# One transformer block on one core: where a weight half is loaded, which engine reads a norm first, how a turned tile lies in PSUM, and how the last tile is stored

## The chip, the cores and the metric

The kernel runs on one core of a Trainium2 chip, in one launch. The metric is the device time of one execution in microseconds; of several runs the median is given. The profile is of one execution, taken apart by engine: TensorE (PE for its matmuls, PEld for its weight loads, which overlap them), VectorE (DVE), ScalarE (ACT), GpSimd (POOL), and SyncE (SP), which here only issues DMA transfers.

## The reference, cut to what matters

One block with 2048 tokens of width 576: a modulated layer norm, linear attention with 32 heads of width 18 and a two-sided softmax feature map, a gated residual; then a second modulated norm, a feed-forward of width 4608 with a relu, and a gated residual.

```python
mod = (silu(c) @ w_mod).reshape(1, 6, 1, -1)
sa, ca, ga, sb, cb, gb = (mod[:, i] for i in range(6))
h = layernorm(x) * (1 + ca) + sa
# attention, per head: q, k, v = h @ wqkv
pq, pk = q @ w_phi, k @ w_phi
phi_q = concat([softmax(pq), softmax(-pq)]);  phi_k = concat([softmax(pk), softmax(-pk)])
kv, z = phi_k.T @ v, phi_k.sum(over tokens)
o = (phi_q @ kv) / (phi_q @ z + 1e-6)
x = x + ga * (o @ wo)
h = layernorm(x) * (1 + cb) + sb
x = x + gb * (relu(h @ w1) @ w2)
```

## The kernel before

The tokens are 16 tiles of 128. The first phase is a list of short jobs, issued in a fixed order that is written down as a string of words. A word is a job, the number of its tile or chunk, and after a colon the pair of PSUM banks it uses (`Q12:3`: query projection of tile 12 into bank pair 3). Each engine does its own jobs in the order of the words. The ones the text speaks of:

- `K`, `V`, `Q`: projections (10 matmuls each); `eK`, `eQ`: the exponentials (ScalarE) that evacuate them; `sK`, `rK`, `pA`, `pM`, `vE`, `kv`: the key side; `FQ..`, `QR..`: folding the feature weights into the query weights, and their bias rows
- `sq`, `qi`: spill of a query tile to DRAM, and its reload; `qs`, `qp`, `qt`: its sums (VectorE), its second half (GpSimd), its turning by DMA
- `ga`, `gac`, `gaw`, `gar`: the attention gate as a row, written to DRAM and read back to all partitions; `wo`: the output weight times this row (GpSimd, five chunks)
- `nu`, `nO`, `ot`, `oc`: attention numerator of tile 0 or 1, its division, its turning and evacuation; `W`: output projection with the residual added
- `lb`, `lr`, `ap`: statistics, inverse deviation and application of the second norm; `xc`: copy of the residual out of PSUM; `ht`, `hd`, `ha`: turning of the normed tile, and evacuation with scale and shift by VectorE and ScalarE
- `wl`, `w2a`, `w2b`: loads of the feed-forward weights

The end of the string, where the query tiles and the first two attention tiles meet, reads before the change:

```python
... nu0:3 eQ6 Q7:2 sq5 nO0 sq4 nu1:1 eQ7 ot0:0 w2b1 nO1 Q8:3 oc0 Q9:2 eQ8 sq7 W0:1
eQ9 sq8 ot1:0 sq6 lb0 xc0 Q10:3 oc1 w2b0 lr0 Q11:2 eQ10 ap0 W1:0 eQ11 sq10 w2b2 ht0:1 lb1 xc1 Q12:3 ha0 hd0
lr1 Q13:2 eQ12 ap1 qi3 Q14:1 eQ13 sq11 ht1:0 sq12 Q15:3 ha1 hd1 sq13 eQ14 sq9 sq14 qi4 eQ15 sq15
```

The query tiles share six buffers, so tile 15 takes that of tile 9 after its spill; the reload `qi3` takes the buffer of tile 10:

```python
SLOT = (0, 1, 2, 3, 4, 5, 0, 1, 2, 3, 4, 5, 0, 1, 2, 3)
EL = carve(RT, RTL, (NL, 2 * D))          # its first two buffers are slots 4 and 5
def q_out(u): sp.dma_start(eqd[:, u, :], EQ[:, SLOT[u], :])
def q_in(u):  sp.dma_start(EL[:, u % NL, :], eqd[:, u, :])
def exps(t, pr, E):                       # eQ: two of them for each tile
    for s in range(2):
        act.activation(out=..., in_=pr[:, :, 0:HD]..., func=ACT.Exp, scale=rs[:, t, s:s + 1])
```

The second half of the second weight lies in a buffer `R2[1]` which first holds the transposed x of tiles 0 to 7:

```python
XOFF[t0 + j] = (R2[1], off, nt, j) if t0 < 8 else (RT, ...)      # x^T, 5120 of 10368 columns
def w2b_part(k):                                                  # three loads
    c = slice(6 * k * D, 6 * (k + 1) * D)
    sp.dma_start(R2[1][:, c], a["w2b"][:, c])
```

Turning and evacuating a normed tile:

```python
def turn(src, pr):
    pt = bf(pr[:, 0, :])                                          # one bank
    for ci in range(NC):
        pe.transpose(pt[:, ci * P:(ci + 1) * P], src[:, ci * P:(ci + 1) * P], ident[:, 0:P])

def h2_e(i, pr, eng):
    pt = bf(pr[:, 0, :])
    for ci in range(NC):
        o, p = h2[:, 0, ci, i * P:(i + 1) * P], pt[:, ci * P:(ci + 1) * P]
        if ci % 2 and eng is act:
            act.activation(out=o, in_=p, func=ACT.Identity, scale=..., bias=...)
        elif ci % 2 == 0 and eng is dve:
            dve.tensor_scalar(out=o, in0=p, scalar1=..., scalar2=..., op0=ALU.mult, op1=ALU.add)
```

The second phase is eight blocks of two tiles. Each has a first layer (`l1`, three groups of weight columns, each in three steps whose PSUM pairs 0, 1, 2 are evacuated by relus on ScalarE and VectorE) and a second layer (`l2`, seven products of 18 matmuls, a Strassen-like form). Attention and norm of the next two tiles run between their matmuls. The relus and the end of the last block:

```python
def relu(js, u):
    act.activation(out=A11[:, j, :], in_=lo[:, :, 0, :], func=ACT.Relu)
    act.activation(out=A2[:, j, :, :], in_=..., func=ACT.Relu)
    dve.scalar_tensor_tensor(out=U3[:, j, :], in0=lo[:, :, 1, :], scalar=0.0, in1=A11[:, j, :], op0=ALU.max, op1=ALU.subtract)
...
    fin(t + 1, 0, X, None)
    sp.dma_start(outf[(t + 1) * P:(t + 2) * P, :], x_sb[:, t + 1, :])
    prod(Z, A12, B22, al)
    if b + 1 < NB:
        fin(t, 1, Z, 1)
    else:
        y, z, c = yt[:, 0, :], yt[:, 1, :], slice(HD, D)
        pool.tensor_tensor(out=z, in0=SS[:, 1, :], in1=gb_row[:, c], op=ALU.mult)
        pool.tensor_tensor(out=z, in0=z, in1=x_sb[:, t, c], op=ALU.add)
        dve.tensor_tensor(out=y, in0=PS[:, Z, 0:HD], in1=gb_row[:, c], op=ALU.mult)
        dve.tensor_tensor(out=x_sb[:, t, c], in0=y, in1=z, op=ALU.add)
    sp.dma_start(outf[t * P:(t + 1) * P, :], x_sb[:, t, :])
```

Of the kernel before, what the change touches and what calls it, by code (L numbers as in the profile page):

```python
# [7 lines left out]
P = 128  # L8
# [14 lines left out]
NX = X0 + 4  # L23
NJ = DFF // P
HD = 288
G6 = ((0, 6), (6, 6), (12, 4), (16, 6), (22, 6), (28, 4))
GR = 108
GP = 112
# [12 lines left out]


ORDER = """
Z11 sx sd rp sc FK ca Z2 fra2 fsr frd4 fra1 sh fs1 frr fra0 bn0 fs3 bn1 fra3 fs0 Z1 shc sa0 wsd1 KR:0 fsd4 fs2
sp0 bn3 T0:2 VR:1 Tc0 bn2 KRh Ka0:2 KRd sa2 wsd0 sp2 VRh Kb0 wsd3 Ka1:0 wsd4 eKa0 VRd Kb1 wsd2 T2:1 eKa1 sK0
V0:2 Tc2 sK1 FQ1:0 rK0 K3:1 FQra1 pA0 FQs1 pM0 vE0 eK3 K2:0 bn4 bn5 rK1 kv0 eK2 m2:2 pA1 sK3 pM1 sa4 V1:1 sK2
m2c rK3 sp4 FQ3:0 V3:2 pA3 vE1 FQs3 pM3 FQra3 bn6 kv1 rK2 T4:1 V2:0 vE3 Tc4 pA2 bn7 pM2 K4:1 vE2 sa6 bn8 K5:2
eK4 sp6 bn10 T6:0 kv2 Tc6 ga:1 eK5 sK4 K6:0 gac bn9 rK4 V4:2 eK6 pA4 sK5 pM4 K7:1 sa8 vE4 rK5 gb:0 sK6 eK7 pA5
V5:2 sp8 gaw pM5 wl1 bn11 gbc T8:1 rK6 FQ0:0 kv3 Tc8 FQrd0 kv4 sa10 K8:1 pA6 vE5 FQs0 pM6 sK7 kv5 eK8 FQ4:2
V7:0 gar FQrd4 gbw sp10 w2a2 rK7 sK8 K9:1 FQs4 pA7 pM7 vE7 rK8 V6:2 eK9 bn13 gbr wl0 wo2 V8:0 vE6 sK9 pA8 kv6  # L50
kv7 pM8 V9:1 vE8 rK9 bn12 w2a0 T10:2 FQ2:0 pA9 Tc10 kv8 FQrd2 pM9 sa12 K10:2 vE9 FQs2 bn15 QR:1 w2a1 eK10 sp12
K11:0 bn14 wo3 QRh kv9 QRe eK11 V11:2 sK10 wo0 QRd wl3 sa14 T12:1 sK11 wo1 V10:0 Tc12 rK10 pA10 K12:1 rK11
sp14 vE10 pA11 Q0:0 pM10 vE11 eK12 wl4 K13:2 eQ0 sK12 pM11 wl2 kv10 eK13 V13:1 qs0 wo4 rK12 kv11 T14:0 V12:2
sK13 pA12 Tc14 pM12 K14:0 vE12 rK13 pA13 kv12 eK14 vE13 pM13 K15:2 V14:1 sK14 eK15 qp0 kv13 rK14 V15:0 sK15
qt0 pA14 pM14 Q1:2 vE14 rK15 Q2:1 eQ1 pA15 vE15 pM15 kv14 eQ2 Q3:0 qs1 kv15 sq2 eQ3 Q4:2 tp1 qp1 kz sq3 Q5:1
eQ4 qt1 tp0 Q6:0 eQ5 tp2 qi2 nu0:3 eQ6 Q7:2 sq5 nO0 sq4 nu1:1 eQ7 ot0:0 w2b1 nO1 Q8:3 oc0 Q9:2 eQ8 sq7 W0:1
eQ9 sq8 ot1:0 sq6 lb0 xc0 Q10:3 oc1 w2b0 lr0 Q11:2 eQ10 ap0 W1:0 eQ11 sq10 w2b2 ht0:1 lb1 xc1 Q12:3 ha0 hd0
lr1 Q13:2 eQ12 ap1 qi3 Q14:1 eQ13 sq11 ht1:0 sq12 Q15:3 ha1 hd1 sq13 eQ14 sq9 sq14 qi4 eQ15 sq15
"""

@with_exitstack
def tile_block(ctx, tc, a, out):
    nc = tc.nc
    outf = out.flatten_outer_dims()
# [49 lines left out]
    ident = small([P, P + 1], BF16, "ident")  # L114
# [9 lines left out]
    gb_row = small([P, D], BF16, "gb_row")  # L124
# [11 lines left out]
    sc = small([P, 4, NX], BF16, "sc")  # L136
# [19 lines left out]
    PS = psum.tile([P, 8, 512], FP32, name="PS")  # L156
# [6 lines left out]
    act, dve, pool, sp, pe = nc.scalar, nc.vector, nc.gpsimd, nc.sync, nc.tensor  # L163

    def bf(ap):
        return ap.bitcast(BF16)

    XOFF = {}
    off = 0
    for t0, nt in BLK:  # L170
        for j in range(nt):
            XOFF[t0 + j] = (R2[1], off, nt, j) if t0 < 8 else (RT, off - 8 * NC * P + xT_hi, nt, j)
        off += NC * nt * P

    def xt(t, ck, n=1):
# [277 lines left out]

    w1a = carve(R1, 0, (4, DFF))
    w1b = R1[:, 4 * DFF:]
    NK = NJ // 2
    w2 = [carve(R2[i], 0, (NK, D)) for i in range(2)]
    B11, B21, B22 = w2[0][:, :, 0:HD], w2[1][:, :, 0:HD], w2[1][:, :, HD:D]
    B12, T3 = w2[0][:, :, HD:D], carve(R2[0].bitcast(FP16), 0, (NK, D))[:, :, HD:D]
    RTh = RT.bitcast(FP16)  # L460
    T1, T2, T4 = (carve(RTh, i * TW, (NK, HD)) for i in range(3))
# [3 lines left out]
    A12, A22 = A2[:, :, 0, :], A2[:, :, 1, :]  # L465
    SS = RS[:, 0:6 * HD].bitcast(FP32).rearrange("p (a f) -> p a f", f=HD)
    X, Y, Z = 6, 4, 7
# [58 lines left out]
    def turn(src, pr):  # L526
        pt = bf(pr[:, 0, :])
        for ci in range(NC):
            pe.transpose(pt[:, ci * P:(ci + 1) * P], src[:, ci * P:(ci + 1) * P], ident[:, 0:P])

    def h2_e(i, pr, eng):
        pt = bf(pr[:, 0, :])
        for ci in range(NC):
            o, p = h2[:, 0, ci, i * P:(i + 1) * P], pt[:, ci * P:(ci + 1) * P]
            if ci % 2 and eng is act:
                act.activation(out=o, in_=p, func=ACT.Identity, scale=mod2[:, 1, ci:ci + 1], bias=mod2[:, 0, ci:ci + 1])
            elif ci % 2 == 0 and eng is dve:
                dve.tensor_scalar(out=o, in0=p, scalar1=mod2[:, 1, ci:ci + 1], scalar2=mod2[:, 0, ci:ci + 1],  # L538
                                  op0=ALU.mult, op1=ALU.add)

# [2 lines left out]
        sp.dma_start(R2[0][:, c], a["w2a"][:, c])  # L543

    def w2b_part(k):
        c = slice(6 * k * D, 6 * (k + 1) * D)
        sp.dma_start(R2[1][:, c], a["w2b"][:, c])

    def w1_part(i):
# [39 lines left out]
    def k_minus(t):  # L589
# [9 lines left out]
    at = {}  # L599
# [12 lines left out]
                                         in1=ca1[0:R, :].unsqueeze(2).to_broadcast([R, NC, FW]), op=ALU.mult),  # L612
# [23 lines left out]
        "W": lambda i: wo_mm(i, at["W", i], True), "lb": lambda i: ln2_bn(i, at["W", i]), "lr": ln2_rs,  # L636
        "xc": lambda i: act.activation(out=v2(x_sb[:, i, :]), in_=at["W", i][:, :, 0:HD], func=ACT.Copy),
        "ap": lambda i: ln2_apply(i, at["W", i]),
        "ht": lambda i: turn(xn[:, i, :], at["ht", i]),
        "hd": lambda i: h2_e(i, at["ht", i], dve), "ha": lambda i: h2_e(i, at["ht", i], act),  # L640
        "tp": lambda k: t_part(0, k),
    }
# [70 lines left out]
    def fin(t, k, bank, s):  # L713

        c = slice(k * HD, (k + 1) * HD)
        y = yt[:, k, :]
        if s is None:
            dve.tensor_tensor(out=y, in0=PS[:, bank, 0:HD], in1=gb_row[:, c], op=ALU.mult)  # L718
        else:
            dve.tensor_tensor(out=y, in0=PS[:, bank, 0:HD], in1=SS[:, s, :], op=ALU.add)  # L720
            pool.tensor_tensor(out=y, in0=y, in1=gb_row[:, c], op=ALU.mult)  # L721
        pool.tensor_tensor(out=x_sb[:, t, c], in0=y, in1=x_sb[:, t, c], op=ALU.add)  # L722

    def l2(b, hooks):
# [24 lines left out]
        copy(1)
        prod(Z, A11, T1, lo, True)  # L750
        prod(X, U3, T3, al)
        copy(2)
        prod(Z, A11, T1, hi)
        if b == 0:
            dve.tensor_tensor(out=A12, in0=A12, in1=U2, op=ALU.subtract)
        fin(t + 1, 1, Z, 2)
        prod(X, A22, T4, al)
        fin(t + 1, 0, X, None)
        sp.dma_start(outf[(t + 1) * P:(t + 2) * P, :], x_sb[:, t + 1, :])
        prod(Z, A12, B22, al)  # L760
        if b + 1 < NB:
            fin(t, 1, Z, 1)
        else:
            y, z, c = yt[:, 0, :], yt[:, 1, :], slice(HD, D)
            pool.tensor_tensor(out=z, in0=SS[:, 1, :], in1=gb_row[:, c], op=ALU.mult)
            pool.tensor_tensor(out=z, in0=z, in1=x_sb[:, t, c], op=ALU.add)
            dve.tensor_tensor(out=y, in0=PS[:, Z, 0:HD], in1=gb_row[:, c], op=ALU.mult)
            dve.tensor_tensor(out=x_sb[:, t, c], in0=y, in1=z, op=ALU.add)
        sp.dma_start(outf[t * P:(t + 1) * P, :], x_sb[:, t, :])

    NB = NT // 2
    for b in range(NB):
        t0 = 2 * b + 2
# [144 lines left out]
```

The softmax here doesn't subtract the row's maximum and nothing guards it: scores larger than these inputs give would overflow.

## Time and profile before

| | before |
|---|---|
| time, median of 3 runs | 395.94 us (395.25 to 397.05) |
| span of the profiled execution | 396.0 us |
| first layer of block 0 starts | 96.88 us |
| second layer of block 0 starts | 117.57 us |
| last matmuls end | 391.9 us |
| `w2b` loads, x count, size, median time to land | x3, 864 KB, 8.5 us |
| spills of query tiles | x14, 288 KB, 3.6 us |
| stores of output tiles | x16, 144 KB, 1.7 us |

The page gives busy time per engine first. Matmuls overlap one another, so a stretch in which PE shows as busy throughout may still hold slow spots: the distance between the starts of equal pieces tells more than the busy share. In a timeline a piece is a run of equal instructions, with the idle time of its engine ahead of it and what ended that idle time in brackets. A wait matters only if TensorE, which has next to no idle time, stands at the end of it. The DMA list gives the time from issue to landing; issues on the sync queue go out in order, so one that must wait holds back all behind it.

### The profile page before, as it was taken

To read this page: it belongs to the slowest core of one execution; us is meant where nothing else is said; L and a number is where in the kernel's file an instruction comes from. 1 tells how busy PE (TensorE), PEld (TensorE's weight loads), DVE (VectorE), ACT (ScalarE), POOL (GpSimd) and SP (SyncE) were. 2 spreads that over 40 slices of the span, in tenths; PEclk is the share of its full clock that TensorE was granted. 3 is DMA by queue.
4 is the path that set the end of the run, shared out by engine and by line. 5 is a ranking of instruction groups with operands and counts; after the bars stand their busy time and mean duration, and the time that the engine had idled before them with its cause. 6 is when DMAs were issued, how large, how long until landed. Compare 5 with 4: busy or idle time off the path is not lost.

```text
span 396.0 us, 8920 instructions
## 1 busy us (share of the span) xinstructions
PE 384.5 (97%) x3698; PEld 311.1 (79%) x3698; DVE 243.8 (62%) x452; ACT 157.6 (40%) x360; POOL 141.6 (36%) x199
## 2 busy tenths in 40 slices
PE   7999999998899999999999999999999999999995
PEld 3778888876687888788878888887888778878884
DVE  0799997845489845754657376557655755654221
ACT  1788877787441053113312411341053113312510
POOL 2145889600201420651074026404520651072045
PEclk9999999999999999999999999999999999999999
DMA  8999777398641142025212411341141045110000
GB/s 233 346 390 362 259 278 290 91 304 289 190 104 34 31 106 65 18 59 118 25 33 62 108 36 31 88 73 29 40 98 35 17 56 63 26 34 31 2 0 31
DMA packets 49468, 44.41 MB, mean 112 GB/s; under 512 B 39362, under 2 KB 41907, under 8 KB 48915
## 3 DMA queue, kind: packets, MB, share of 16 engines
q1 hardware_dynamic: 49154, 43.66, 39.0%
q8 instruction: 29, 0.48, 0.5%
q10 hardware_dynamic: 272, 0.18, 0.2%
q14 instruction: 13, 0.10, 0.1%
HBM read 28.03 MB, written 6.49 MB: 87 GB/s over the span
## 4 chain that ended last, share of the span: by engine, by line
PE 78%; DMA 7%; POOL 7%; ACT 3%; DVE 2%; issue 2%; SPq 0%; POOLq 0%; ACTq 0%; DVEq 0%
PE PS L676 31%; PE PS L735 29%; PE PS L273 6%; PE PS L683 4%; PE PS L409 4%; DMA eqd<-RT 3%; DMA R<-in_wkT_dram 2%; ACT RT L278 2%; POOL RT L290 2%; PE PS L390 1%; POOL wo_sb L630 1%; DMA R<-in_w2a_dram 1%; POOL RH L747 1%; DMA RE<-RT 1%; DVE st L240 1%
## 5 line engine op out<-in xcount | busy, mean ns | idle before, releaser
L676 PE MATMUL PS<-h,R 128*128 128x256 bf16 x1152 | 134.0, 273 | 2.3 <-DVE RH L692 1.2
L676 PEld LDWEIGHTS <-R 128*128 128x128 bf16 x1152 | 109.8, 98 | 20.5 <-issue 8.1
L735 PEld LDWEIGHTS <-RH 128*128 128x128 f16 x864 | 84.5, 98 | 21.8
L721 POOL TENSOR_TENSOR yt<-yt,gb_row 128x288 f32<-128x288 f32 x23 | 16.8, 730 | 165.6 <-DVE yt L720 165.6
L735 PE MATMUL PS<-R,RH 128*128 128x288 bf16 (+1 forms) x576 | 75.6, 286 | 0.0
L690 ACT ACTIVATE RH<-PS 128x256 f16<-128x256 f32 x72 | 27.6, 384 | 112.7 <-PE PS L683 106.2
L692 DVE SCALAR_TENSOR_TENSOR RH<-PS,RH 128x256 f16<-128x256 f32 x72 | 30.1, 419 | 68.3 <-ACT RH L690 68.3
L278 ACT ACTIVATE RT<-PS,rs 128x576 bf16<-128x576 f32 x64 | 43.1, 742 | 9.7 <-DMA eqd<-RT 5.1
L691 ACT ACTIVATE RH<-PS 128x512 f16<-128x512 f32 x72 | 43.0, 597 | 7.5 <-PE PS L676 6.2
L739 ACT ACTIVATE RS<-PS 128x288 f32<-128x288 f32 x24 | 9.8, 410 | 75.9 <-PE PS L735 75.9
L735 PE MATMUL PS<-RT,RH 128*128 128x288 f16 x288 | 37.9, 286 | 0.0
L273 PE MATMUL PS<-RH,R 116*128 116x288 bf16 x240 | 32.0, 286 | 0.6 <-ACT RH L624 0.5
L273 PE MATMUL PS<-RH,RT 116*128 116x288 bf16 x240 | 32.3, 286 | 0.1
L747 POOL TENSOR_TENSOR RH<-RH,RT 128x2304 f16<-128x2304 f16 x7 | 31.8, 4548 | 0.0
L273 PEld LDWEIGHTS <-R 116*128 116x128 bf16 x240 | 22.8, 98 | 6.7 <-issue 0.9
L273 PEld LDWEIGHTS <-RT 116*128 116x128 bf16 x240 | 22.6, 98 | 5.8 <-DVE h L538 0.4
L419 DVE TENSOR_SCALAR xn<-x_sb,mv,rs 128x576 bf16<-128x576 bf16 (+1 forms) x28 | 22.4, 841 | 7.3 <-ACT rs L414 7.3
L722 POOL TENSOR_TENSOR x_sb<-yt,x_sb 128x288 bf16<-128x288 f32 x31 | 22.7, 734 | 6.6 <-DVE yt L718 4.8
L240 DVE BATCH_NORM_STATS2 st<-x_sb 128x6 f32<-128x288 bf16 x60 | 24.2, 446 | 0.5
L409 PE MATMUL PS<-wo_sb,oT 128*128 128x288 bf16 x160 | 22.5, 286 | 0.0
L283 DVE TENSOR_REDUCE Rk<-RT 128x64 f32<-128x1152 bf16 x16 | 21.2, 1339 | 1.6 <-ACT RT L278 1.6
L345 POOL TENSOR_TENSOR ratq<-Rq,rq 128x32 f32<-128x32 f32 x16 | 4.9, 307 | 48.0 <-DVE rq L342 47.4
(115 smaller groups left out, 428.9 us busy)
## 6 DMA issues: line engine op xcount, KB each, us to landing
R<-in_w1a_dram SPq DMA_DIRECT2D x4, 1152.0 KB, 8.7
eqd<-RT SPq DMA_DIRECT2D x14, 288.0 KB, 3.6
RT<-eqd SPq DMA_DIRECT2D x14, 288.0 KB, 2.8
R<-in_w2a_dram SPq DMA_DIRECT2D x3, 864.0 KB, 10.8
R<-in_w2b_dram SPq DMA_DIRECT2D x3, 864.0 KB, 8.5
out_dram<-x_sb SPq DMA_DIRECT2D x16, 144.0 KB, 1.7
RT<-in_xT_dram SPq DMA_DIRECT2D x2, 640.0 KB, 14.3
x_sb<-in_xk_dram SPq DMA_DIRECT2D x3, 288.0 KB, 9.8
```

The costliest lines, as they stand in the source:

```text
L240: dve.bn_stats(out=s[:, hf, :], in_=x_sb[:, t, hf * HD:(hf + 1) * HD])
L273: pe.matmul(pr[:, k, 0:HD], lhsT=xt(t, ck), rhs=w[0:R, ck, k * HD:(k + 1) * HD], start=(ck == 0), stop=(ck == NC - 1))
L278: act.activation(out=E.rearrange("p (b h s e) -> p b h s e", b=2, s=2, e=DH)[:, :, :, s, :], in_=pr[:, :, 0:HD].rearrange("p b (h e) -> p ...
L409: pe.matmul(pr[:, k, 0:HD], lhsT=oT[:, t % 2, ci, :], rhs=wo_sb[:, ci, k * HD:(k + 1) * HD], start=(ci == 0 and not add_x), stop=(ci == NC ...
L419: dve.tensor_scalar(out=o, in0=i, scalar1=mv[:, 1, t, 0:1], scalar2=rs2[:, t, 0:1], op0=ALU.subtract, op1=ALU.mult)
L676: pe.matmul(PS[:, 2 * u + hf, n * 256:n * 256 + 256], lhsT=w1a[:, ci, jj * P:(jj + 1) * P], rhs=hb[:, ci, :], start=(n == 0 and ci == 0), ...
L690: act.activation(out=A11[:, j, :], in_=lo[:, :, 0, :], func=ACT.Relu)
L691: act.activation(out=A2[:, j, :, :], in_=PS[:, 2 * u + 1, :].rearrange("p (n s f) -> p n s f", n=2, s=2), func=ACT.Relu)
L692: dve.scalar_tensor_tensor(out=U3[:, j, :], in0=lo[:, :, 1, :], scalar=0.0, in1=A11[:, j, :], op0=ALU.max, op1=ALU.subtract)
L722: pool.tensor_tensor(out=x_sb[:, t, c], in0=y, in1=x_sb[:, t, c], op=ALU.add)
L735: pe.matmul(PS[:, bank, 0:HD], lhsT=am[:, j, :], rhs=bm[:, j, :], start=first and j == 0, stop=(j % 9 == 8), skip_group_check=True)
L747: pool.tensor_tensor(out=A12, in0=A12, in1=U2, op=ALU.subtract)
```

## The change: what it does and what it is for

Four things are changed, and the order of the words is written anew with them. The loads of the second weight half are two instead of three; x^T of the first tiles moves to the upper half of the buffer, so that the lower load need not wait for the queries of these tiles. The residual copy `xc` stands behind the application of the norm `ap`. The five turned chunks are spread over both banks of their pair, even ones in one, odd ones in the other, so that VectorE and ScalarE each have a bank. The last tile is stored in two halves of 288 columns, the first as soon as it is there.

```diff
-XOFF[t0 + j] = (R2[1], off, nt, j) if t0 < 8 else ...
+XOFF[t0 + j] = (R2[1], NK * HD + off, nt, j) if t0 < 8 else ...
 def w2b_part(k):
-    c = slice(6 * k * D, 6 * (k + 1) * D)
+    c = slice(NK * HD * k, NK * HD * (k + 1))

+def turn2(src, pr):
+    for ci in range(NC):
+        c = slice(ci // 2 * P, ci // 2 * P + P)
+        pe.transpose(bf(pr[:, ci % 2, :])[:, c], src[:, ci * P:(ci + 1) * P], ident[:, 0:P])
 def h2_e(i, pr, eng):
-    pt = bf(pr[:, 0, :])
-    for ci in range(NC):
+    odd = int(eng is act)
+    pt = bf(pr[:, odd, :])
+    for n, ci in enumerate(range(odd, NC, 2)):
...
-"ht": lambda i: turn(xn[:, i, :], at["ht", i]),
+"ht": lambda i: turn2(xn[:, i, :], at["ht", i]),
...
+rows, z = slice(t * P, (t + 1) * P), yt[:, 1, :]                 # last block alone
+sp.dma_start(outf[rows, 0:HD], x_sb[:, t, 0:HD])
+pool.tensor_tensor(out=z, in0=SS[:, 1, :], in1=gb_row[:, HD:D], op=ALU.mult)
+pool.tensor_tensor(out=z, in0=z, in1=x_sb[:, t, HD:D], op=ALU.add)
 prod(Z, A12, B22, al)
...
-sp.dma_start(outf[t * P:(t + 1) * P, :], x_sb[:, t, :])
+sp.dma_start(outf[rows, HD:D], x_sb[:, t, HD:D])
```

The order of the words from the early load on, with cuts marked (the whole list is new, but keeps its kinds and counts except for one `w2b` less):

```diff
+... FQ4:2 kv7 pM9 FQrd0 kv8 FQrd4 V9:1 FQs0 w2b0 bn13 FQs4 QR:0 vE9 K11:2 ...
+... vE14 rK15 kv13 V15:1 qs1 pA15 gar pM15 kv14 Q2:2 vE15 qp1 kv15 eQ2 Q3:0 tp0 wo4 qt1 kz Q4:1 eQ3 wo2 sq2
+tp2 Q5:2 eQ4 sq3 tp1 wo3 nu0:3 eQ5 Q6:0 sq4 nO0 wo0 qi2 Q7:1 eQ6 wo1 sq5 ot0:2 w2b1 eQ7 nu1:3 Q8:0 nO1 oc0
+Q9:1 eQ8 W0:3 eQ9 sq7 lb0 ot1:2 sq8 Q10:0 oc1 sq6 lr0 W1:1 ap0 eQ10 sq9 lb1 xc0 ht0:2 sq10 Q11:0 ha0 hd0 lr1
+Q12:3 eQ11 ap1 Q13:2 qi3 xc1 eQ12 sq11 ht1:0 Q14:1 hd1 ha1 sq12 eQ13 Q15:3 qi4 eQ14 sq13 eQ15 sq14 sq15
```

More of the change, by code (lines that the diff above doesn't have):

```diff
@@ L25 @@
 HD = 288
+NK = NJ // 2
 G6 = ((0, 6), (6, 6), (12, 4), (16, 6), (22, 6), (28, 4))
@@ L43 @@
 ORDER = """
[L44 to L58, printed above, removed]
+Z11 sx sd rp sc FK ca Z2 fs0 fsr frr fra2 sh frd4 fra0 fra1 bn1 fs3 bn0 fs1 Z1 fra3 shc sa0 wsd2 KR:0 fsd4 fs2
@@ new lines @@
+sp0 bn2 T0:2 VR:1 KRh bn3 Tc0 Ka0:2 KRd sa2 wsd1 sp2 VRh Kb0 wsd0 Ka1:0 wsd4 eKa0 VRd Kb1 wsd3 T2:1 eKa1 sK0
+V0:2 Tc2 sK1 FQ3:0 rK0 K3:1 FQra3 pA0 FQs3 pM0 vE0 eK3 K2:0 bn4 bn5 rK1 kv0 eK2 FQ1:2 pA1 V1:1 sK3 pM1 FQra1
+m2:0 vE1 rK3 sa4 pA3 sK2 FQs1 kv1 sp4 V2:1 m2c pM3 bn7 rK2 T4:2 V3:0 bn6 Tc4 pA2 vE2 pM2 sa6 K4:2 vE3 K5:1
+bn10 eK4 sp6 bn9 T6:0 kv2 Tc6 kv3 eK5 sK4 ga:2 K7:0 gac sK5 rK4 K6:1 eK7 pA4 pM4 bn8 V4:2 eK6 sK7 gb:0 sa8
+V5:1 vE4 wl0 rK7 sp8 rK5 sK6 pA7 T8:2 gbc kv4 pA5 Tc8 FQ2:0 pM5 K8:2 vE5 rK6 FQrd2 K9:1 bn11 eK8 w2a2 pA6 pM6
@@ new lines @@
+bn14 kv5 sa10 V6:2 FQs2 sK8 eK9 sp10 wl1 V7:0 pM7 vE6 rK8 sK9 T10:1 V8:2 Tc10 pA8 vE7 pM8 K10:1 rK9 vE8 w2a0
+kv6 bn12 eK10 FQ0:0 pA9 FQ4:2 kv7 pM9 FQrd0 kv8 FQrd4 V9:1 FQs0 w2b0 bn13 FQs4 QR:0 vE9 K11:2 QRh sa12 QRe
+sK10 sp12 kv9 eK11 V10:1 bn15 QRd wl4 rK10 T12:0 V11:2 sK11 Tc12 pA10 sa14 pM10 K13:0 gbw vE10 rK11 wl2 Q0:1
+pA11 eK13 sp14 vE11 pM11 kv10 eQ0 T14:2 sK13 K12:0 w2a1 Tc14 qs0 kv11 rK13 K14:1 eK12 pA13 pM13 V13:2 eK14
+sK12 wl3 K15:0 qp0 vE13 rK12 sK14 V12:1 eK15 pA12 pM12 qt0 Q1:2 vE12 rK14 sK15 gbr V14:0 pA14 eQ1 gaw pM14
@@ L59 @@
+kv12 vE14 rK15 kv13 V15:1 qs1 pA15 gar pM15 kv14 Q2:2 vE15 qp1 kv15 eQ2 Q3:0 tp0 wo4 qt1 kz Q4:1 eQ3 wo2 sq2
+tp2 Q5:2 eQ4 sq3 tp1 wo3 nu0:3 eQ5 Q6:0 sq4 nO0 wo0 qi2 Q7:1 eQ6 wo1 sq5 ot0:2 w2b1 eQ7 nu1:3 Q8:0 nO1 oc0
+Q9:1 eQ8 W0:3 eQ9 sq7 lb0 ot1:2 sq8 Q10:0 oc1 sq6 lr0 W1:1 ap0 eQ10 sq9 lb1 xc0 ht0:2 sq10 Q11:0 ha0 hd0 lr1
+Q12:3 eQ11 ap1 Q13:2 qi3 xc1 eQ12 sq11 ht1:0 Q14:1 hd1 ha1 sq12 eQ13 Q15:3 qi4 eQ14 sq13 eQ15 sq14 sq15
 """
@@ L171, in tile_block @@
         for j in range(nt):
-            XOFF[t0 + j] = (R2[1], off, nt, j) if t0 < 8 else (RT, off - 8 * NC * P + xT_hi, nt, j)
+            XOFF[t0 + j] = (R2[1], NK * HD + off, nt, j) if t0 < 8 else (RT, off - 8 * NC * P + xT_hi, nt, j)
         off += NC * nt * P
@@ L455, in tile_block @@
     w1b = R1[:, 4 * DFF:]
-    NK = NJ // 2
     w2 = [carve(R2[i], 0, (NK, D)) for i in range(2)]
@@ L529, in turn @@
             pe.transpose(pt[:, ci * P:(ci + 1) * P], src[:, ci * P:(ci + 1) * P], ident[:, 0:P])
+    def turn2(src, pr):
+        for ci in range(NC):
+            c = slice(ci // 2 * P, ci // 2 * P + P)
+            pe.transpose(bf(pr[:, ci % 2, :])[:, c], src[:, ci * P:(ci + 1) * P], ident[:, 0:P])
     def h2_e(i, pr, eng):
-        pt = bf(pr[:, 0, :])
-        for ci in range(NC):
-            o, p = h2[:, 0, ci, i * P:(i + 1) * P], pt[:, ci * P:(ci + 1) * P]
-            if ci % 2 and eng is act:
+        odd = int(eng is act)
+        pt = bf(pr[:, odd, :])
+        for n, ci in enumerate(range(odd, NC, 2)):
+            o, p = h2[:, 0, ci, i * P:(i + 1) * P], pt[:, n * P:(n + 1) * P]
+            if odd:
                 act.activation(out=o, in_=p, func=ACT.Identity, scale=mod2[:, 1, ci:ci + 1], bias=mod2[:, 0, ci:ci + 1])
-            elif ci % 2 == 0 and eng is dve:
+            else:
                 dve.tensor_scalar(out=o, in0=p, scalar1=mod2[:, 1, ci:ci + 1], scalar2=mod2[:, 0, ci:ci + 1],
@@ L759, in l2 @@
         sp.dma_start(outf[(t + 1) * P:(t + 2) * P, :], x_sb[:, t + 1, :])
-        prod(Z, A12, B22, al)
[L761 to L769, printed above, removed]
+        if b + 1 < NB:
+            prod(Z, A12, B22, al)
+            fin(t, 1, Z, 1)
+            sp.dma_start(outf[t * P:(t + 1) * P, :], x_sb[:, t, :])
+            return
+        rows, z = slice(t * P, (t + 1) * P), yt[:, 1, :]
+        sp.dma_start(outf[rows, 0:HD], x_sb[:, t, 0:HD])
+        pool.tensor_tensor(out=z, in0=SS[:, 1, :], in1=gb_row[:, HD:D], op=ALU.mult)
+        pool.tensor_tensor(out=z, in0=z, in1=x_sb[:, t, HD:D], op=ALU.add)
+        prod(Z, A12, B22, al)
+        dve.tensor_tensor(out=yt[:, 0, :], in0=PS[:, Z, 0:HD], in1=gb_row[:, HD:D], op=ALU.mult)
+        dve.tensor_tensor(out=x_sb[:, t, HD:D], in0=yt[:, 0, :], in1=z, op=ALU.add)
+        sp.dma_start(outf[rows, HD:D], x_sb[:, t, HD:D])
     NB = NT // 2
```

## The prediction

> **What bounds the kernel now.** I read the page first: busy shares, then the granted clock.
>
> ```profile
> PE 384.5 (97%) x3698; PEld 311.1 (79%) x3698; DVE 243.8 (62%) x452; ACT 157.6 (40%) x360; POOL 141.6 (36%) x199
> ...
> PEclk9999999999999999999999999999999999999999
> ```
>
> TensorE is busy in 384.5 of 396.0 us at full clock, so there are 11.5 us without a matmul, and a change that removes no matmul cannot bring more than a part of them. The changed kernel has the same number of TensorE instructions. The question is therefore where the 11.5 us lie. The table of busy time by window (columns: window, length, then busy time and count of PE, PEld, DVE, ACT, POOL, granted clock, DMA share, GB/s) answers:
>
> ```profile
> 80.00:85.00 5.00, 4.53 (x47) 3.50 (x45) 1.89 (x4) 4.23 (x7) 0.00 (x0) 1.00 1.04 277
> ...
> 95.00:100.00 5.00, 3.95 (x35) 3.10 (x33) 2.46 (x5) 2.12 (x5) 1.42 (x2) 1.00 0.79 267
> 100.00:105.00 5.00, 3.78 (x39) 3.04 (x39) 0.77 (x3) 2.78 (x7) 0.00 (x0) 1.00 0.57 212
> ...
> 136.00:376.00 240.00, 240.00 (x2250) 196.79 (x2249) 137.91 (x263) 71.32 (x167) 78.66 (x74) 1.00 0.26 52
> 376.00:396.00 20.00, 15.92 (x131) 12.52 (x128) 4.63 (x8) 2.08 (x5) 9.56 (x8) 0.96 0.04 16
> ```
>
> From 136 to 376 us there is no gap at all: seven feed-forward blocks follow each other at 37.05 us each (second-layer starts at 117.57, 154.62, 191.67 us in the chain of waits). Nothing in the diff touches them. What can move is the stretch up to about 105 us, and the last 4 us. The start (up to 25 us) lacks about 5 us for its first loads and folds; the order of the words there is nearly the same after the change. So I look at 80 to 105 us, where queries, the first two tiles of attention and the first feed-forward block meet. The timeline there (start, length, engine, line, output<-inputs; in brackets how long the engine had stood and for whom):
>
> ```profile
> 81.15 0.55 PE L390 MATMUL PS<-kvz,RE 128*128 128x76 bf16 x10 [0.47 <-DMA RE<-RT]
> ...
> 95.04 0.82 ACT L536 ACTIVATE h<-PS,mod 128x128 bf16<-128x128 bf16 x2
> 95.24 0.32 SPq L338 DMA_DIRECT2D RT<-eqd  x1
> 95.68 2.73 SPq L335 DMA_DIRECT2D eqd<-RT  x5
> ...
> 95.89 0.85 DVE L538 TENSOR_SCALAR h<-PS,mod 128x128 bf16<-128x128 bf16 x3 [1.98 <-ACT h L536]
> ...
> 96.88 3.22 PE L676 MATMUL PS<-h,R 128*128 128x256 bf16 x28 [1.05 <-DVE h L538]
> ...
> 102.22 1.37 ACT L278 ACTIVATE RT<-PS,rs 128x576 bf16<-128x576 f32 x2 [5.10 <-DMA eqd<-RT]
> ...
> 104.37 3.28 PE L676 MATMUL PS<-h,R 128*128 128x256 bf16 x28 [1.22 <-DVE RH L692]
> ```
>
> Two chains are to be seen. **First**, the turned features of tile 1: TensorE ends its transposes at 94.61, ScalarE takes chunks 1 and 3 from 95.04, and only when it is done VectorE takes 0, 2, 4 from 95.89. TensorE waits 1.05 us for that. **Second**, a load chain: the sync queue issues the last third of the second weight half at 89.76, then stands until 95.24 (a reload needs the buffer of a spill that lies behind the weights). Five spills go out only then; the one of tile 9 (fourth of them, from 97.42 in the chain of waits) lands at 102.2; the exponential of tile 15, which reuses its buffer, waits 5.10 us; the first relus stand behind it on ScalarE, and TensorE waits 1.22 us.
>
> **What the Trainium skill says.** "PSUM — Partial Sum Buffer", section "PSUM bank collisions raise a hardware error": two engines must not touch the same bank (and partition quadrant) at once, reads included, and the compiler's scheduler orders any two that would. The trace agrees: ScalarE and VectorE read disjoint columns of one bank and still go one after the other (0.82, then 0.85 us). "DMA: Bandwidth & Descriptors", section "Queues, rings and completion order": the sync engine has one row of rings, and on each DMA engine descriptors are consumed in ring order. The trace agrees in effect: a 288 KB spill takes a median 3.6 us to land, but 4.7 us behind other traffic at 97.42.
>
> **The change part by part.**
>
> *Turned features in two banks.* Even chunks go to one bank (VectorE), odd ones to the other (ScalarE). No instruction is added; the 0.85 us of VectorE can start with ScalarE's 0.82. With it the order changes: the transposes of tile 1 now stand before the last two query projections (20 matmuls, 2 x 1.23 = 2.46 us by the spacing in the chain of waits), where before there was one. The chunks then need at most 0.85 us plus ScalarE's queue, so the wait of 1.05 us at 96.88 should go. The same evacuation of tile 0 held up a weight load at 92.93 by 0.40 us; counting matmuls, 30 of them took 94.17 - 90.22 = 3.95 us instead of 3.68: 0.27 us to gain.
>
> *Residual copy behind the norm.* Both read one PSUM pair, so before, the norm waited for the copy (0.65 us on ScalarE). It goes off the chain statistics, norm, transposes. By itself it moves no TensorE work: it is what lets the transposes stand earlier. Counted 0.
>
> *Second weight half in two loads.* 3 x 864 KB become 2 x 1296 KB, and the x^T of tiles 0 to 7 moves to the upper half of the buffer, so the lower load can go while projections still run. It is issued ahead of the bias rows of the query weights, by my count of matmuls near 50 us. The queue moved 7.9 MB between 75 and 105 us at a mean of 264 GB/s; 1.33 MB less (1296 KB), at the 0.38 MB per us that its best slices reach (383 to 390 GB/s), is 3.5 us of full rate out of the crowded stretch. The spill of tile 9 now stands ahead of that of tile 10 and of the reload which blocked the queue. It should land near 90 us, well before its buffer is wanted (near 96 us). So the 5.10 us wait on ScalarE goes, and with it the slow first layer of block 0: it took 117.57 - 96.88 = 20.69 us, in block 1 154.62 - 135.54 = 19.08 us. **Gain 1.6 us**, of which 1.22 is the named wait. The earlier load has room: DMA share was 0.37 at 55 to 60 us and 0.40 at 65 to 70.
>
> *Order of the words.* The numerator of tile 1 comes after the turning of tile 0, and the query work of tile 1 on GpSimd comes ahead of the scaling of the output weight; so the wait of 0.47 us at 81.15 should go. The scaling of the output weight (5 x 1.27 us on GpSimd) moves from 48 to 62 us to about 76 to 82 us. Its consumer is at about 84 us: roughly 1.5 us to spare.
>
> *Last tile by halves.* The timeline ends, in a span of 396.0 us, with
>
> ```profile
> 392.62 0.46 DVE L768 TENSOR_TENSOR x_sb<-yt 128x288 bf16<-128x288 f32 x1
> 393.10 0.33 SPq L769 DMA_DIRECT2D out_dram<-x_sb  x1
> ```
>
> The last store falls from 144 to 72 KB. A store takes 1.7 us to land; 72 KB at the 0.38 MB per us above is 0.2 us, the rest is fixed. The GpSimd work ahead of it (until 392.59) keeps its place behind the other tile's. Gain 0.15 us.
>
> Sum: 1.05 + 0.27 + 1.6 + 0.47 + 0.15 = 3.5 us.
>
> **What eats into it.** ScalarE becomes the next limit. Between 80 and 97 us it is busy 15.5 of 17.0 us, TensorE 15.4; the change gives it no less to do there. Eight exponential pairs at 1.33 us (10.6) and 5 us of other pieces make 15.7 us, against 13.9 us of matmuls. If TensorE no longer waits, ScalarE lags by about 2 us at the end. The second group of the first layer needs the bank pair of tile 14; by my count that costs 0.3 us. The whole order was changed, so I expect another 0.3 us in small waits. Net gain 3.5 - 0.6 = 2.9 us: 395.94 - 2.9 = **393.0 us**.
>
> **The rivals.**
> *A. ScalarE takes the place of both waits.* For it: the 91% busy time above. Against: in the first layer there are 3.9 us of matmuls before the first relu is asked for, and 2.3 more before its bank is needed again. If it holds, only 1.5 us are gained: 394.4 us.
> *B. The big loads collide with something else.* The 1296 KB half still goes out after tile 7's queries, ahead of the spills of tiles 7, 8, 6 and 9; the early one delays the first-layer weights and the other w2 third. For it: DMA shares near 1.0 in most windows before 55 us. Against: those weights are read after 95 us. A missed buffer would cost 1 to 3 us: 395 to 397 us.
> *C. GpSimd is late with the output weight.* It waits for a gate row which makes a round trip through DRAM (the other row took 6.1 us to land in the crowded part). At that, the scaling ends 2 to 3 us late and TensorE stands as long: 395 to 396 us. For the opposite: GpSimd was busy 17.6 of 20 us from 40 to 60 us, and freeing it there helps the key side. But TensorE lost almost nothing there, so I add nothing.
>
> **Range and chances.** Best case is the full sum and a little of the start: 391.3. Rivals B or C alone give 396. I take 391.3 to 396.0. A gain of 2% needs 388.0, twice the sum; a loss of 2% (403.9) needs a stall that none of these steps has.
>
> **What would show it.** In the changed profile: both h pieces (ScalarE, VectorE) overlap in time, and the first layer's first matmul has no wait over 0.3 us and starts near 94.9 us; no exponential waits over 1 us for a spill; first layer of block 0 takes 19.1 to 19.5 us; blocks still 37.05 us; one w2b load near 50 us, landing far before use; end after the last store about 0.2 us shorter. The prediction is wrong if TensorE shows new waits between 25 and 85 us, on the scaled output weight or on key and value evacuations, or if ScalarE's lag holds the first layer.

## The result, and the profile after

The changed kernel takes 393.56 us (median; 393.07 to 393.81) against 396.25 us: ratio 0.9932, 95% interval 0.9906 to 0.9958, so 2.7 us less. Two further comparisons beside the experiments gave 0.9908 (0.9873 to 0.9942) and 0.9914 (0.9890 to 0.9939). The prediction was 393.0 us.

The page of the changed kernel, first part (busy time, share of the span, instructions of each engine):

```profile
PE 383.3 (98%) x3697; PEld 311.2 (79%) x3698; DVE 244.9 (63%) x452; ACT 157.9 (40%) x360; POOL 142.4 (36%) x199
```

TensorE's busy time is the same within 1.2 us; its time without a matmul falls from 11.5 to 391.6 - 383.3 = 8.3 us. The table of busy time by window shows where (columns as before: PE, PEld, DVE, ACT, POOL, granted clock, DMA share, GB/s):

```profile
75.00:80.00 5.00, 4.36 (x43) 3.31 (x40) 4.97 (x5) 4.84 (x8) 5.00 (x3) 1.00 0.98 298
...
95.00:100.00 5.00, 5.00 (x52) 4.11 (x51) 1.07 (x3) 3.91 (x8) 1.19 (x2) 1.00 0.78 260
100.00:105.00 5.00, 5.00 (x52) 4.12 (x51) 3.72 (x6) 1.85 (x4) 1.42 (x2) 1.00 0.69 139
...
132.00:373.00 241.00, 241.00 (x2261) 197.84 (x2259) 138.46 (x265) 72.15 (x168) 78.57 (x74) 1.00 0.26 52
```

From 95 to 105 us, where 2.3 us were lost, TensorE now has no gap. A new gap stands between 75 and 80 us, where TensorE was busy throughout before (5.00 us), and where GpSimd and VectorE are both full. The timeline of the changed kernel names the pieces:

```profile
74.76 7.83 POOL L637 TENSOR_TENSOR wo_sb<-wo_sb,ga_row 128x576 bf16<-128x576 bf16 x5 [1.59 <-DMA ga_row<-gatd]
74.93 4.07 DVE L474 TENSOR_TENSOR RT<-R 128x1728 f16<-128x1728 bf16 x2
...
80.12 0.45 PE L529 MATMUL PS<-ident,o_sb 128*128 128x128 bf16 x5 [0.76 <-DVE o_sb L399]
...
80.84 7.30 SPq L336 DMA_DIRECT2D eqd<-RT  x5
...
91.33 0.32 SPq L339 DMA_DIRECT2D RT<-eqd  x1
...
92.20 0.85 DVE L545 TENSOR_SCALAR h<-PS,mod 128x128 bf16<-128x128 bf16 x3 [1.60 <-PE PS L535]
92.43 0.83 ACT L543 ACTIVATE h<-PS,mod 128x128 bf16<-128x128 bf16 x2
...
94.38 3.22 PE L683 MATMUL PS<-h,R 128*128 128x256 bf16 x28
...
97.96 0.38 ACT L697 ACTIVATE RH<-PS 128x256 f16<-128x256 f32 x1 [0.90 <-PE PS L690]
...
113.55 1.26 PE L742 MATMUL PS<-R,RH 128*128 128x288 bf16 x9
```

The h pieces of VectorE and ScalarE overlap (92.20 and 92.43). Both end before the first layer starts at 94.38 without a wait in brackets. The five spills (tiles 7, 8, 6, 9, 10) are issued before the reload at 91.33, and ScalarE's first relu (97.96) waits for TensorE, not for a spill; no exponential waits for one either. The first layer takes 113.55 - 94.38 = 19.17 us (20.62 us before by the same lines, from 96.88 to 117.50). What is new is the wait of 0.76 us at 80.12: GpSimd's scaling of the output weight and VectorE's two weight differences run side by side from 74.9 us on, and the attention division of tile 0, which TensorE waits for, stands behind these differences. The early load, which no line here shows, went out at 39.77 us.

Executions differ by up to 2 us in when their first weights land. To compare stages I count from the start of the first fold matmul of each execution. "A" is the start of the first layer of block 0, "B" that of its second layer, both from that point; "end" is from the issue of the last store to the end of the span.

| kernel | A | B | end | ratio to before (95% interval) |
|---|---|---|---|---|
| before | 86.76 | 107.38 | 2.90 | 1 |
| after, first profile | 85.36 | 104.53 | 2.72 | 0.9932 (0.9906 to 0.9958) |
| after_again | 84.76 | 103.93 | 2.67 | 0.9908 (0.9873 to 0.9942) |
| e1, two banks alone | 85.32 | 105.53 | 2.90 | 1.0019 (0.9993 to 1.0045) |
| e2, spill of tile 9 earlier alone | 86.51 | 105.68 | 2.86 | 0.9986 (0.9962 to 1.0011) |
| e4, both | 85.47 | 104.64 | 2.91 | 0.9950 (0.9924 to 0.9975) |
| a1, after with one bank | 84.75 | 104.33 | 2.75 | 0.9897 (0.9849 to 0.9944) |
| a2, after with the late load | 85.56 | 104.98 | 2.75 | 0.9945 (0.9916 to 0.9975) |
| a4, after, differences behind the divisions | 84.42 and 85.43 | 103.59 and 104.60 | 2.72 and 2.69 | 0.9888 (0.9829 to 0.9947), 0.9918 (0.9894 to 0.9941) |
| a3, after without the gate scaling | 84.43 | 103.60 | 2.73 | one run |
| a5, after with the copy first | 84.97 | 104.13 | 2.68 | one run |

From B on all kernels are alike: 275.3 to 275.7 us up to the last store. The profiled executions of e3 and after_five had a lower TensorE clock from 10 to 25 us (0.57 and 0.89); they are left out of the table.

### The profile page after: what moved, and what is told of

Same layout as the page of the kernel before. It is cut to its first block, busy times and chain, and to the rows that moved or that the text cites. A ratio compares the mean times of both kernels' runs of the same rounds, so it can differ in the third digit from the quotient of the medians.

```text
span 391.6 us, 8916 instructions
## 1 busy us (share of the span) xinstructions
PE 383.3 (98%) x3697; PEld 311.2 (79%) x3698; DVE 244.9 (63%) x452; ACT 157.9 (40%) x360; POOL 142.4 (36%) x199
## 4 chain that ended last, share of the span: by engine, by line
PE 89%; DVE 4%; POOL 2%; DMA 2%; ACT 1%; issue 1%; SPq 0%; POOLq 0%; DVEq 0%; ACTq 0%
PE PS L683 33%; PE PS L742 29%; PE PS L274 12%; PE PS L410 5%; PE PS L690 5%; DMA R<-in_wkT_dram 2%; PE PS L324 1%; PE PS L391 1%; POOL RH L754 1%; DVE RT L474 1%; DVE st L241 1%; ACT RT L279 1%; POOL x_sb L729 1%; PE PS L438 0%; POOL yt L728 0%
## 5 line engine op out<-in xcount | busy, mean ns | idle before, releaser
L284 DVE TENSOR_REDUCE Rq<-RT 128x64 f32<-128x1152 bf16 x16 | 21.5, 1343 | 0.0
```

Of the source, the lines that this page charges most:

```text
L284: dve.tensor_reduce(out=Rr, in_=E.rearrange("p (c e) -> p c e", e=DH), axis=AXX, op=ALU.add)
```

## The experiments

**e1: two banks alone.** In the kernel before:

```diff
-"ht": lambda i: turn(xn[:, i, :], at["ht", i]),
+"ht": lambda i: turn2(xn[:, i, :], at["ht", i]),      # and h2_e as in the change
```

> The kernel before with the turned features in two PSUM banks, and nothing else. My theory (two chains that end at the same place): the wait of 1.05 us ahead of the first layer falls below 0.3 us and it starts about 0.9 us earlier, but the exponential of tile 15 still waits for its spill until the same moment, so the relu wait of 1.2 us grows to about 2.1 us and the second layer of block 0 starts where it did: 396.2 us, within 0.3 us of before. Rival (the gains of the parts add): 0.9 us faster, 395.3 us.

The timeline of e1:

```profile
92.47 0.85 DVE L545 TENSOR_SCALAR h<-PS,mod 128x128 bf16<-128x128 bf16 x3 [0.81 <-PE PS L535]
92.90 0.82 ACT L543 ACTIVATE h<-PS,mod 128x128 bf16<-128x128 bf16 x2
...
93.49 3.22 PE L683 MATMUL PS<-h,R 128*128 128x256 bf16 x28
...
98.42 1.38 ACT L278 ACTIVATE RT<-PS,rs 128x576 bf16<-128x576 f32 x2 [3.44 <-DMA eqd<-RT]
...
100.58 3.28 PE L683 MATMUL PS<-h,R 128*128 128x256 bf16 x28 [0.82 <-DVE RH L699]
```

The two evacuations overlap and A moves by 86.76 - 85.32 = 1.44 us, more than my 0.9. The exponential still waits for its spill (3.44 us) and TensorE still stands at the second group (0.82 us). The time did not fall: ratio 1.0019 (0.9993 to 1.0045). In this one profile, which is of the fastest of its 20 executions (393.87 us), B is 1.85 us earlier, because the spill landed sooner in it (98.42 is 90.25 us after the first fold; 92.10 us before). So the second half of my statement, that the relu wait grows to 2.1 us, did not hold in the profiled execution, while the time says that hardly anything was gained (at most 0.3 us, by the interval). How long that wait is depends on when the spill lands, and that varies.

**e2: the spill of tile 9 earlier.** One word moved in the kernel before:

```diff
-... ot1:0 sq6 lb0 ... qi3 ... sq13 eQ14 sq9 sq14 ...
+... ot1:0 sq6 sq9 lb0 ... qi3 ... sq13 eQ14 sq14 ...
```

> The kernel before with one word moved: the spill of tile 9 is issued behind that of tile 6, ahead of the second w2b load, instead of behind the reload that blocks the queue. My theory (the place of this spill in the queue is what cost 1.6 us): no exponential waits over 1 us for a spill, first layer of block 0 takes 19.1 to 19.5 us instead of 20.7, the wait of 1.05 us ahead of it stays: 394.7 us. Rival (the weight traffic itself is the cause, and only the early load cures it): the spill lands late all the same, and the time stays at 396.2 us.

The timeline of e2:

```profile
88.40 0.42 SPq L547 DMA_DIRECT2D R<-in_w2b_dram  x1
...
92.84 0.32 SPq L338 DMA_DIRECT2D RT<-eqd  x1
...
95.28 3.22 PE L676 MATMUL PS<-h,R 128*128 128x256 bf16 x28 [0.82 <-DVE h L538]
...
114.45 1.26 PE L735 MATMUL PS<-R,RH 128*128 128x288 bf16 x9
```

The mechanism is as I said: with all weight loads still late, and the reload still held up (to 92.84), no exponential waits for a spill. The first layer takes 114.45 - 95.28 = 19.17 us, and the wait on the h pieces stays at 0.82 us. The size is not: B is 1.70 us earlier than in the profile before, but the ratio of the times is 0.9986 (0.9962 to 1.0011), at most 1.5 us, by its middle 0.6. The profiled execution of before was not a typical one: it took 397.95 us, 2 us over the median of 395.94. About 1 us or more of this lies ahead of the first fold matmul, which started at 10.12 us there and at 8.17 to 9.15 us in all other profiles. The timeline of before, then that of e2:

```profile
10.12 1.79 PE L437 MATMUL PS<-RS,R 108*116 108x108 bf16 x30 [0.91 <-DMA R<-in_wkT_dram]
```

```profile
8.77 1.79 PE L437 MATMUL PS<-RS,R 108*116 108x108 bf16 x30 [0.39 <-DMA R<-in_wkT_dram]
```

The rest can be the wait for the spill. With the landing of e1's profile, 1.85 us sooner, TensorE would not have waited at the second group of before. This is an estimate from the two profiles: the group could have started 94.25 - 1.85 = 92.40 us after the first fold, and TensorE was free at 94.25 - 1.22 = 93.03 us. The table under e4 shows how far the executions spread.

**e3: the weight half early, the spill late.** In the kernel before, x^T moved up and the loads in two halves:

```diff
-... bn12 w2a0 T10:2 ... w2b1 ... w2b0 ... w2b2 ...
+... bn12 w2a0 w2b0 T10:2 ... w2b1 ...
```

> The kernel before with the w2b load in two halves, the lower one ahead of the bias rows of the query weights, x^T moved as in the change; the spill of tile 9 keeps its late place. My theory (place in the queue): the reload still blocks the queue until the spill of tile 10 has landed, but that lands sooner with less traffic, near 92 to 93 us instead of 95.2; the spill of tile 9 lands near 99 us, the exponential waits 1 to 3 us, and TensorE's relu wait is nearly gone: 394.8 us. Rival (only the order of spills matters): the wait of 5.1 us and the time of 396.2 us stay.

The timeline of e3:

```profile
101.15 3.22 PE L676 MATMUL PS<-h,R 128*128 128x256 bf16 x28 [0.96 <-DMA eqd<-RT]
...
103.90 1.38 ACT L278 ACTIVATE RT<-PS,rs 128x576 bf16<-128x576 f32 x2 [2.51 <-DMA eqd<-RT]
```

The exponential of tile 15 waits 2.51 us instead of 5.10, inside the 1 to 3 us I expected, and no relu wait is left at TensorE; the wait ahead of the first layer stays (0.96 us). But the ratio is 0.9995 (0.9968 to 1.0022), where I expected 394.8 us (0.9965). In the profile the first layer starts 92.0 us after the first fold matmul, 5 us later than before, which gives the transfers more time, so it can't decide. What the early load does by itself stays open here; a2 says more.

**e4: two banks and the earlier spill.**

> The kernel before with two banks and the earlier spill of tile 9 together, weight loads as before. My theory: with the spill out of the way the two banks now pay, first layer of block 0 starts 0.9 us earlier and takes 19.1 to 19.5 us; the sum of 0.9 and 1.5 us: 393.8 us, as fast as the whole change within 0.5 us. Rival (ScalarE becomes the limit, one of the two waits comes back as another): no more than the better of the two alone, 394.7 us or above.

A 85.47, B 104.64, first layer 19.17 us, no wait on either chain: 0.9950 (0.9924 to 0.9975), 2.0 us. By the middles of the intervals they bring more together than the sum of what either brought alone (nothing and 0.6 us): alone, each leaves TensorE a wait of 0.82 us on the other's chain. The rival, ScalarE as the new limit, is refuted: from 80 to 97 us its profile has no gap at TensorE, with ScalarE busy 15.7 of 17.0 us. The table of busy time by window for e4:

```profile
80.00:97.00 17.00, 17.00 (x156) 13.89 (x155) 8.82 (x20) 15.72 (x30) 1.42 (x2) 1.00 0.93 333
```

The times of this comparison, over the executions with a granted clock of 0.999 or 1.0 alone, beside the wait of an exponential for its spill in the one profile of each kernel:

| kernel | executions | median, us | range, us | wait for the spill, us |
|---|---|---|---|---|
| before | 46 | 395.64 | 394.41 to 397.95 | 5.10 |
| e1 | 5 | 396.20 | 394.97 to 397.85 | 3.44 |
| e3 | 9 | 395.28 | 394.39 to 396.41 | 2.51 |
| e2 | 9 | 394.79 | 394.48 to 395.46 | none |
| e4 | 11 | 393.95 | 393.31 to 394.43 | none |

Where an exponential waits for the spill, the times spread over 2 to 3.5 us; where it does not, over 1.0 to 1.1 us. So this wait seems to have another length in each execution; taking it away takes most of the spread away. By the medians the earlier spill alone brings 0.85 us and both parts 1.7 us. The whole change brings 2.95 us by the same measure (after_five, 393.05 against 396.00 us), so I was wrong to expect e4 as fast as the change within 0.5 us. The missing 1 us or so is divided among the early load, the new order and the halved store; only a2 takes one of them apart.

**after_again and after_five: the change unaltered.**

> The changed kernel unaltered, as the standard for the runs beside it. 393.5 us; first layer of block 0 starts 85.4 us after the first fold matmul and takes 19.2 us; the turning of tile 0's attention output waits 0.7 us for VectorE.

> The changed kernel unaltered, in more rounds: 393.4 us, ratio to before 0.992; the first layer starts 84.8 to 85.4 us after the first fold matmul, according to whether GpSimd or VectorE comes first at their shared access.

The timeline of after_again:

```profile
74.73 3.09 DVE L474 TENSOR_TENSOR RT<-R 128x1728 f16<-128x1728 bf16 x2
...
75.17 7.49 POOL L637 TENSOR_TENSOR wo_sb<-wo_sb,ga_row 128x576 bf16<-128x576 bf16 x5 [2.20 <-DMA ga_row<-gatd]
...
82.71 0.65 PE L410 MATMUL PS<-wo_sb,oT 128*128 128x288 bf16 x4 [0.19 <-POOL wo_sb L637]
```

Ratios 0.9908 and 0.9914. In after_again the wait at 80 us is gone, and one of 0.19 us for the output weight stands in its place; A is 84.76 instead of 85.36. In the first profile GpSimd began 0.17 us ahead of VectorE, and the two differences took 4.07 us; here VectorE began first, and they took 3.09 us. GpSimd begins when the gate row has landed: 65.74 us after the first fold in the first profile, 66.33 us here. The profiles of after_five, a1, a2 and a5 went like this one, with 0.18 to 0.20 us. So the landing of the row seems to decide which engine goes first, and the wait of 0.76 us is the rarer case, one of six. The A of after_five, 86.16 us, is beyond what I expected, but its lower clock from 10 to 25 us lengthened it by an unknown part.

**a1: one bank again.**

```diff
-"ht": lambda i: turn2(xn[:, i, :], at["ht", i]),
+"ht": lambda i: turn(xn[:, i, :], at["ht", i]),       # and h2_e as before
```

> The changed kernel with the turned features back in one bank, order of words kept. My theory (the two query projections that now follow the transposes, 2.46 us, hide the serial evacuation): the first layer's first matmul waits less than 0.3 us, ScalarE is 0.6 us later at its end, and the time is 0.0 to 0.4 us above the changed kernel, 393.7 us. Rival (the two banks are what brought the 1.05 us): the wait returns and the time is 0.8 to 1.2 us higher, 394.5 us.

The timelines of a1, VectorE and ScalarE, then TensorE:

```profile
91.42 0.85 DVE L544 TENSOR_SCALAR h<-PS,mod 128x128 bf16<-128x128 bf16 x3 [1.25 <-PE PS L529]
...
92.36 0.81 ACT L542 ACTIVATE h<-PS,mod 128x128 bf16<-128x128 bf16 x2 [0.24 <-DVE h L544]
...
93.59 1.91 PE L682 MATMUL PS<-h,R 128*128 128x256 bf16 x16
95.75 1.47 PE L682 MATMUL PS<-h,R 128*128 128x256 bf16 x12 [0.24 <-ACT RT L279]
```

The pieces go one after the other again, A stays (84.75 against 84.76), and ScalarE is later by 0.7 us, for which TensorE pays at the second group: 0.24 us by the bracket, 0.40 us in B (104.33 - 103.93). The times can't tell 0.4 us (0.9897, interval 0.0095 wide). So there are two cures for the 1.05 us: two banks (e1), or the new order, by my theory through the two projections behind the transposes (a1). The change has both; for this wait one is enough, while the two banks still spare ScalarE the 0.7 us.

**a2: both weight halves late.**

```diff
-... V9:1 FQs0 w2b0 bn13 ... ot0:2 w2b1 eQ7 ...
+... V9:1 FQs0 bn13 ... ot0:2 w2b1 w2b0 eQ7 ...
```

> The changed kernel with both w2b halves loaded after the queries of tile 7, order of words kept otherwise. My theory (the place of the spills carries the gain, the early load is only insurance): no exponential waits over 1 us for a spill; spills land some 3 us later and the time is 0 to 0.6 us above the changed kernel, 393.8 us. Rival (the early load carries it): exponentials or the sums of the first layer wait 1 to 3 us for spills, 395 us or above.

The timeline of a2:

```profile
91.38 1.38 ACT L279 ACTIVATE RT<-PS,rs 128x576 bf16<-128x576 f32 x2 [1.21 <-DMA eqd<-RT]
...
92.81 1.39 PE L274 MATMUL PS<-RH,RT 116*128 116x288 bf16 x10 [0.63 <-ACT RT L279]
```

An exponential does wait, 1.21 us, and TensorE 0.63 us for it; B is 1.05 us later than in after_again (104.98 - 103.93). By the middles of the ratios it is 1.5 us slower (0.9945 against 0.9908). The intervals (0.9916 to 0.9975 and 0.9873 to 0.9942) overlap, but all 11 executions of a2, from 393.84 us on, lie above all six of after_again, which ran in the same comparison (up to 393.68). My theory allowed 0.6 us, so it fell short: the early load is no mere insurance, it carries 1 to 1.5 us of the gain, with the order that the change has.

**a3: without the gate scaling** (it leaves out the product of the output weight with the attention gate).

```diff
-"wo": lambda c: pool.tensor_tensor(out=wo_sb[:, c, :], in0=wo_sb[:, c, :], in1=ga_row[:], op=ALU.mult),
+"wo": lambda c: None,
```

> The changed kernel without the scaling of the output weight by the gate row (it leaves the attention gate out, so its output differs). My theory (GpSimd's scaling slows VectorE's weight differences, and these hold up the attention division): the second and third part of the difference take about 1.1 us each instead of 1.5 to 2.0, TensorE has no wait at the turning of tile 0 nor for the output weight, and the first layer starts 84.3 to 84.6 us after the first fold matmul. Rival (the transfers into these buffers slow VectorE): the two parts still take 1.5 to 2.0 us each.

VectorE's two differences in the changed kernel are in its timeline above (74.93). The scaling in it (by tile: shortest, median and longest in ns), and the timeline of a3:

```profile
L637 POOL TENSOR_TENSOR wo_sb<-wo_sb,ga_row x5: 1266/1275/2087, 74.8 to 81.3; 128x576 bf16<-128x576 bf16 x5
```

```profile
74.80 2.01 DVE L474 TENSOR_TENSOR RT<-R 128x1728 f16<-128x1728 bf16 x2
...
93.32 3.22 PE L683 MATMUL PS<-h,R 128*128 128x256 bf16 x28
```

Two differences take 2.01 us together without the scaling, and 4.07 us with it. A is 84.43; at the turning and at the output projection TensorE has no wait left. So one difference takes about 1.0 us alone and about 2.0 us against a product, and one product 1.27 or 2.09 us, as if the one that comes second stood until the other is through. "SBUF — State Buffer" in the Trainium skill, section "SBUF: two separate sides", says this of a VectorE instruction with two SBUF inputs and a GpSimd instruction that reads SBUF, as both do here: "whichever [...] starts first gets the pair for the whole instruction; the other fully blocks". The numbers agree: the surplus is 0.8 to 1.1 us, most of one instruction of the other engine. The rival (transfers) fell: in a3 the transfers are issued as before, and the surplus is gone.

**a4: the two differences behind the divisions.** In the changed kernel:

```diff
-... Q4:1 eQ3 wo2 sq2 tp2 Q5:2 eQ4 sq3 tp1 wo3 ... nO0 wo0 ... nO1 oc0 ...
+... Q4:1 eQ3 wo2 sq2 Q5:2 eQ4 sq3 wo3 ... nO0 tp1 wo0 ... nO1 tp2 oc0 ...
```

> The changed kernel with two VectorE jobs (second and third part of the first weight difference, 2 us each there) moved behind the two attention divisions. My theory (these jobs, slowed by GpSimd's scaling of the output weight, hold up the division and so TensorE by 0.8 us): the wait at the turning of tile 0 falls below 0.2 us, and the first layer starts 0.4 to 0.7 us earlier: 392.9 us. Rival (the wait only moves, to the scaled output weight or to the statistics of the norm): first layer starts where it did, within 0.2 us, 393.5 us.

> The changed kernel with the two VectorE jobs behind the attention divisions, a second time in more rounds, beside the changed kernel. My theory: the first layer of block 0 starts near 84.4 us after the first fold matmul every time, because the collision of these jobs with GpSimd no longer stands ahead of TensorE: 392.7 us, ratio to before 0.990. Rival (the first time was luck of the loads): same as the changed kernel, 393.4 us, ratio 0.992.

In the first profile the wait was gone and A 84.42. In the second VectorE's differences took little longer than alone (1.08 and 1.25 us), GpSimd's scaling 0.8 us longer than in the first (7.83 against 7.03 us), and the gate row had landed 0.45 us later (66.66 against 66.21 us after the first fold). So the scaling ended late, and TensorE stood for it. The timeline of the second:

```profile
75.49 7.83 POOL L637 TENSOR_TENSOR wo_sb<-wo_sb,ga_row 128x576 bf16<-128x576 bf16 x5 [2.52 <-DMA ga_row<-gatd]
...
83.38 0.65 PE L410 MATMUL PS<-wo_sb,oT 128*128 128x288 bf16 x4 [0.84 <-POOL wo_sb L637]
```

A is 85.43 there. So my "every time" was wrong: the wait moves, as the rival said. With ratios of 0.9888 and 0.9918 and wide intervals a4 isn't shown to be faster than the change.

**a5: the copy ahead of the norm.**

```diff
-... sq6 lr0 W1:1 ap0 eQ10 sq9 lb1 xc0 ht0:2 ... hd0 lr1 ... qi3 xc1 eQ12 ...
+... sq6 xc0 lr0 W1:1 ap0 eQ10 sq9 lb1 ht0:2 ... hd0 xc1 lr1 ... qi3 eQ12 ...
```

> The changed kernel with the residual copy ahead of the norm again, order otherwise kept. My theory (statistics, norm and transposes of tile 0 are one chain with no slack, as the transposes start 0.2 us after the norm): the transposes of tile 0 come 0.5 to 0.7 us later, TensorE waits that long there, nothing more for tile 1: first layer starts 0.5 to 0.7 us later. Rival (counted 0 in the prediction: the copy lies beside other work): within 0.2 us of the changed kernel.

A is 84.97 and B 104.13, 0.2 us later than after_again, less than the 0.5 to 0.7 us that I expected here. In the changed order the copy's place is worth about 0.2 us; one run each, so even that is not certain.

## Why the prediction was right, step by step

- **What bounds it:** right. From B on nothing moved (275.3 to 275.7 us); the gain lies before B and after the last store.
- **The wait of 1.05 us and the 0.27 us of tile 0:** gone. e1 shows 1.44 us in A for the two banks alone. In the times they bring nothing alone, and 0.84 us once the spill is early (e4 against e2, by the medians). The prediction gave this to the banks with the order's help; a1 shows that the order alone removes the wait too.
- **The first layer of block 0:** predicted 19.1 to 19.5 us, measured 19.17. But the 1.6 us were taken from one profile in which the spill landed late. Removed by itself (e2), the wait is worth 0.6 us by the middle of the ratio and 0.85 us by the medians at one clock. So this term of the sum was too large. The early load, booked within it, carries 1 to 1.5 us when the order is that of the change (a2), because there an exponential waits again without it. It went out at 39.77 us, not near 50; the count of matmuls was off, and no run shows that it mattered.
- **0.47 us at 81.15:** gone, and replaced. The step that failed is "Its consumer is at about 84 us: roughly 1.5 us to spare". GpSimd had the gate row at 74.76 us (its load took 3.0 us), earlier than the 76 us expected, but its five products and VectorE's differences held one another up: the products took 7.83 us instead of 5 x 1.27. TensorE waited 0.76 us in one profile and 0.18 to 0.20 us in five others. New waits before 85 us, on the scaled output weight too, were the prediction's own sign of being wrong, and in this one step it was. Rival C named the right job, but as a late row, not as a collision with VectorE, and its 2 to 3 us did not come.
- **Last tile by halves:** 0.15 us predicted; the end takes 2.86 to 2.91 us with whole stores (five profiles) and 2.67 to 2.75 us with halves (nine): 0.2 us.
- **ScalarE's lag of 0.3 us:** not seen in the changed kernel, whose first layer has no wait. It shows only once a1 adds 0.7 us to ScalarE.

The first profiles bear out the stages: (86.76 - 85.36) + (20.62 - 19.17) + 0.2 = 3.05 us, where 3.5 were summed before the deductions. The deductions were 0.3 us for a lag of ScalarE, which did not come, and 0.3 us for small waits. Together they covered what the prediction had not seen, an oversized term for the spill and a collision that cost 0.2 to 0.8 us. That the total came out within 0.6 us is in part luck.

## What to carry to other kernels

When two chains hold up the same engine one after the other, curing one may show little or nothing: try them together before calling either useless. When issues go out in order, as on the sync queue here, the place of a small spill can matter as much as the traffic; look at which issue stands, and what stands behind it. And the length of a wait on a transfer can differ from one execution to the next: compare the time of the profiled execution with the median, and see in which stage the surplus lies, before its length goes into a sum.

## What the runs showed of the hardware that was not expected

Two ordinary elementwise operations, a difference on VectorE (1.0 us) and a product on GpSimd (1.27 us), on tensors that have nothing to do with each other, took up to 2.1 us when they met (the two differences, 2.0 us together without the products, took 3.1 or 4.1 us with them). Which of them pays more changed from execution to execution of the same kernel. And the spills and reloads of one size (288 KB) between 60 and 120 us in the changed kernel landed after 2.3 to 7.7 us, median 3.7.
